# Half-swaps of the last four batches issued from GpSimd's queue instead of the sync queue

## Chip, core and metric

The kernel runs on one NeuronCore of a Trainium2 chip. Its engines work side by side, each through its own instruction queue: TensorE (PE, with PEld for its weight loads), VectorE (DVE), ScalarE (ACT), GpSimd (POOL) and SyncE (SP). SP, ACT and POOL can issue DMAs, and a queue is worked off in order. The metric is the time of one execution in microseconds (us), lower being better; the profile is one such execution, with the time of each instruction.

## Reference

Eight batches of 576 rows and 8 heads of 64 go through a Performer attention; the heads are laid side by side to 512 channels and go through a Hyena block, whose convolution runs over the 576 rows.

```python
def _attn_ref(q, k, v, omega):
    scale = 1.0 / np.sqrt(np.sqrt(D))
    q_s, k_s = (q * scale, k * scale)
    ...
    q_p, k_p = (phi(q_s), phi(k_s))          # 128 random features
    kv = np.einsum('bhsm,bhsd->bhmd', k_p, v)
    z = np.sum(k_p, axis=2)
    num = np.einsum('bhsm,bhmd->bhsd', q_p, kv)
    den = np.einsum('bhsm,bhm->bhs', q_p, z)[..., None] + 1e-06
    return num / den

def _moe_ref(x, w_proj, filter_fft, w_out):
    proj = x @ w_proj                         # 512 -> 3 * 512
    x1, x2, x3 = ...
    X2 = np.fft.rfft(x2, n=S, axis=1)
    H = np.fft.rfft(filter_fft, n=S, axis=0)[None, :, :]
    x2_conv = np.fft.irfft(X2 * H, n=S, axis=1)
    return (x1 * x2_conv * x3) @ w_out
```

## The kernel before

Each batch has 512 rows in four tiles of 128; the 64 rows left over of two batches are worked together, so the batches go in four pairs, `i` from 0 to 3, with `bb` 0 and 1 in a pair. Attention (DVE, ACT and PE) runs ahead of the Hyena stages, and the stages of different batches overlap.

In `hyena()` a pair passes these stages. `fold` makes sums and differences of row chunks, and `project2` multiplies them by the middle third of `wproj`. `forward` takes the Fourier transform by matmuls with tables (`fwb`, `fwa` and others), whose results ScalarE casts to bf16 tiles: `xs` for one part of the spectrum and `sp` for the other. `spectrum` multiplies by the filter on VectorE, and the inverse stage goes back by matmuls that have columns of `xs`, `sp` and `xr` as weights. `gates` makes x1 times x3, and `out` multiplies by `wout`; results are scaled by ScalarE into `osb` (or spare) tiles and stored by SP.

In `sp`, and in `xr` for the left rows of a pair, the two terms of a complex number lie in the two partition halves (0 to 63 and 64 to 127). The complex product therefore needs each half beside the other: `sw` is a copy of `sp` with its halves swapped, and `xw` one of `xr`. Each copy is two DMAs from SBUF to SBUF of 64 partitions: 128 KB for a half of `sw` by the profile's count, 64 KB for a half of `xw`. On VectorE `sp` is multiplied by `hps`, `sw` by `hqs`, and the two are added into `sp`. The first of these overwrites `sp`, so it waits for the swaps too, which read it. `xr`, `xw` work in the same way in `left_spectrum`. There are two buffers of `sw` and of `sp`, one of `xr` and of `xw`.

All instructions are first recorded in a list, then issued in the order of the table `ORDER`, written out in the file, of which every engine gets its own part in that order; the profile puts them all on line 247, the place that issues them, so they are told apart here by tile names. Before the change SP has the loads of a few constants, all swaps and all output stores but one, mixed as `ORDER` has them: a swap that waits for ScalarE's cast holds up the stores behind it, and the reverse. POOL has the loads of q, k, v and the weights, of which the last begins at 137.74 us.

The copies of a pair stand in the functions below.

Of the kernel before, what the change touches and what calls it, by code (L numbers as in the profile page):

```python
# [250 lines left out]
def kernel(  # L251
# [11 lines left out]
    nc = Plan(tc.nc, tc)  # L263
# [31 lines left out]
    def bank():  # L295
        ps = nc.tile(psum, [P, 512], FP32, name="h", bufs=4)
        nc.banks[ps.tensor.name] = ps
        return ps
# [96 lines left out]
    for j in range(2):  # L395
        nc.vector.tensor_scalar_mul(
            out=om2[j * D : (j + 1) * D, :], in0=omt[:D, :MF], scalar1=qk_scale
# [35 lines left out]
    lo64, hi64 = slice(0, 64), slice(64, 128)  # L433
# [619 lines left out]
    def hyena():  # L1053
# [60 lines left out]
        def spectrum(xs, sp, sw):  # L1114
            bt = nc.tile(hy, [P, 2, DM], BF16, name="bt", bufs=2)
            nc.vector.tensor_tensor(
                out=bt[:], in0=xs[:], in1=hb[:].unsqueeze(1).to_broadcast([P, 2, DM]), op=ALU.mult
            )
            nc.vector.tensor_tensor(
                out=xs[:], in0=xs[:], in1=ha[:].unsqueeze(1).to_broadcast([P, 2, DM]), op=ALU.mult  # L1120
            )
            nc.vector.tensor_tensor(
                out=xs[:, 0, :], in0=xs[:, 0, :], in1=bt[:, 1, :], op=ALU.subtract
            )
            nc.vector.tensor_tensor(
                out=xs[:, 1, :], in0=xs[:, 1, :], in1=bt[:, 0, :], op=ALU.add
            )
            nc.vector.tensor_tensor(out=sp[:], in0=sp[:], in1=hps[:, 0:2], op=ALU.mult)
            nc.vector.tensor_tensor(out=sw[:], in0=sw[:], in1=hqs[:, 0:2], op=ALU.mult)
            nc.vector.tensor_tensor(out=sp[:], in0=sp[:], in1=sw[:], op=ALU.add)  # L1130
# [5 lines left out]
        for i in range(B // 2):  # L1136
# [24 lines left out]
            for bb in range(2):  # L1161
# [4 lines left out]
                out=pf[:],  # L1166
# [5 lines left out]
            for j in range(2):  # L1172
                nc.tensor.matmul(
                    out=pf[:],
# [5 lines left out]
            xr = nc.tile(hy, [P, DM], BF16, name="xr", bufs=1)  # L1180
            xw = nc.tile(hy, [P, DM], BF16, name="xw", bufs=1)
            nc.scalar.copy(out=xr[:], in_=pf[:])
            nc.sync.dma_start(out=xw[lo64], in_=xr[hi64])
            nc.sync.dma_start(out=xw[hi64], in_=xr[lo64])

            def left_spectrum():
                nc.vector.tensor_tensor(out=xr[:], in0=xr[:], in1=hps[:, 2], op=ALU.mult)
                nc.vector.tensor_tensor(out=xw[:], in0=xw[:], in1=hqs[:, 2], op=ALU.mult)
                nc.vector.tensor_tensor(out=xr[:], in0=xr[:], in1=xw[:], op=ALU.add)
# [3 lines left out]
            def forward(bb):  # L1193
                nc.at("forward", 2 * i + bb)
                x2 = x2s[bb]
                xs = nc.tile(hy, [P, 2, DM], BF16, name="xs", bufs=2)
                sp = nc.tile(hy, [P, 2, DM], BF16, name="sp", bufs=2)
                xss.append(xs)
                sps.append(sp)
                for m in (2, 3, 0, 1):  # L1200
                    pf = bank()
                    if m < 3:
                        for kt_ in (2, 0, 1):
                            nc.tensor.matmul(
                                out=pf[:],
                                lhsT=fwb[:, 3 * m + kt_, :],
                                rhs=x2[:, kt_, :],
                                start=(kt_ == 2),
                                stop=(kt_ == 1),
                            )  # L1210
                    else:
                        nc.tensor.matmul(
                            out=pf[:], lhsT=fwar[:, bb, :], rhs=x2l[:], start=True, stop=False
                        )
                        nc.tensor.matmul(
                            out=pf[:], lhsT=fwa[:], rhs=x2[:, 3, :], start=False, stop=True
                        )
                    nc.scalar.copy(
                        out=xs[:, m, :] if m < 2 else sp[:, m - 2, :], in_=pf[:]
                    )  # L1220
                    if m == 3:
                        sw = nc.tile(hy, [P, 2, DM], BF16, name="sw", bufs=2)
                        nc.sync.dma_start(out=sw[lo64], in_=sp[hi64])
                        nc.sync.dma_start(out=sw[hi64], in_=sp[lo64])
                spectrum(xs, sp, sw)
                if bb == 0:
                    left_spectrum()
            for bb in range(2):
                forward(bb)
# [8 lines left out]
            for pp, off in ((p1, 0), (p3, 2 * DM)):  # L1238
                for nb in range(CB):
                    for ct in range(CB):  # L1240
                        nc.tensor.matmul(
                            out=pp[:, nb * P : (nb + 1) * P],
# [8 lines left out]
                out=x13l[:].rearrange("p n b s -> p (n b s)"), in0=p3[:], in1=x1[:], op=ALU.mult  # L1251
# [4 lines left out]
            for bb in range(2):  # L1256
                nc.at("inverse", 2 * i + bb)
                xs, sp = xss[bb], sps[bb]
                yt = nc.tile(hy, [P, CB, SM], BF16, name="yt", bufs=2)
                yts.append(yt)  # L1260
                for g in range(CB // 2):
                    gs = slice(2 * g, 2 * g + 2)
                    pa = bank()
                    for u in range(2):
# [3 lines left out]
                            out=dst, lhsT=sp[:, 1, ns], rhs=gta[:, 0:CH], start=True, stop=False  # L1268
                        )
                        nc.tensor.matmul(  # L1270
                            out=dst, lhsT=xr[:, ns], rhs=gns[:, bb, 0:CH], start=False, stop=True
# [8 lines left out]
                    for terms in (  # L1280
# [12 lines left out]
                        for u in range(2):  # L1293
                            ns = slice((2 * g + u) * P, (2 * g + u + 1) * P)
                            for n_, (l_, r_) in enumerate(terms(ns)):
                                nc.tensor.matmul(
                                    out=pv[:, u, 0:EC], lhsT=l_, rhs=r_, start=(n_ == 0), stop=(n_ == 1)
# [5 lines left out]
                        out=yw[:, :, 0], in0=odd[:, :, 0:CH], in1=yc[:, :, 0:CH], op=ALU.add  # L1303
                    )
                    nc.vector.tensor_tensor(
                        out=yw[:, :, 1],
# [5 lines left out]
                        out=yw,  # L1312
# [6 lines left out]
                        out=yt_[:, :, 0:CH], in0=yw[:, :, 0], in1=yw[:, :, 1], op=ALU.add  # L1319
                    )  # L1320
                    nc.vector.tensor_tensor(
                        out=y[:, :, 5::-5],
# [6 lines left out]
                        out=yt[:, gs], in0=x13s[bb][:, gs], in1=yf[:, :, 0:SM], op=ALU.mult  # L1329
                    )  # L1330
                    nc.vector.tensor_tensor(
                        out=ytl[:, gs, bb], in0=x13l[:, gs, bb], in1=yf[:, :, SM:S], op=ALU.mult
# [8 lines left out]
            for bb in range(2):  # L1341
# [5 lines left out]
                for t in order:  # L1347
# [7 lines left out]
                    if final:  # L1355
                        for k_, cs in enumerate((slice(0, 384), slice(384, DM))):
                            n_ = cs.stop - cs.start
                            po = bank()
                            for nb in range(CB):
                                nc.tensor.matmul(  # L1360
                                    out=po[:, 0:n_],
# [8 lines left out]
                            else:  # L1370
                                nc.vector.tensor_scalar(
                                    out=osb,
# [6 lines left out]
                                out=out[b, t * P : (t + 1) * P, cs], in_=osb  # L1379
# [3 lines left out]
                    for nb in range(CB):  # L1383
                        nc.tensor.matmul(
                            out=po[:],
# [12 lines left out]
                    else:  # L1398
                        for j in range(2):
                            nc.sync.dma_start(  # L1400
                                out=out[2 * i + j, SM:S, :], in_=osb[j * SL : (j + 1) * SL, :]
                            )

    attention()
    hyena()
    with tc.nc.allow_low_precision(reason="bf16 factors of both sums"), tc.manual_schedule():
        nc.issue()
# [31 lines left out]
```

## Time and profile before

| | |
|---|---|
| time, median of 3 runs | 261.37 us (260.96 to 261.98) |
| the profiled execution's own time | 261.67 us |
| its span, first to last instruction | 259.9 us |
| mean granted TensorE clock | 0.993 |
| DMAs that POOL issues, software queue q0 | 59616 packets, 17.31 MB |
| DMAs that SP issues, queue q1 | 8280 packets, 12.68 MB |
| swaps issued by SP | 16 of `sw` (median 2.5 us from issue to landing), 8 of `xw` (2.0 us) |
| output stores of 256 KB issued by SP | 24 from `osb`, 2.3 us to landing |

Times in views of the profile count from the first instruction. A line of the timeline gives start, length, engine, source line, operation, tile written and read, and in brackets the idle time before it with what ended it. A line of a stretch gives busy time and number of instructions of each engine in it. The chain of waits is followed back from the last instruction, at each step to what released it.

### The profile page before, as it was taken

What the parts mean: (1) busy time and instruction counts of PE and PEld (TensorE: products, weight loads), DVE (VectorE), ACT (ScalarE), POOL (GpSimd) and SP (SyncE); (2) the same over time, 40 slices, a digit from 0 to 9 for tenths busy, and PEclk for the clock granted to TensorE, in tenths of its full rate; (3) what the DMA queues carried; (4) which work ended last, traced back from release to release, by engine and by line L of the source; (5) the groups of instructions that cost most, each with busy time, mean ns of one, the idle gap of its engine ahead of it and who ended that gap; (6) DMA issues with size and microseconds to landing.
All of it is one profiled execution on the core that took longest, in us unless ns stands there. A gap on an engine that the chain in (4) does not pass through costs nothing.

```text
span 259.9 us, 6421 instructions
## 1 busy us (share of the span) xinstructions
PE 249.1 (96%) x2564; PEld 152.9 (59%) x2564; DVE 219.7 (85%) x501; ACT 214.3 (82%) x334; POOL 62.7 (24%) x87
## 2 busy tenths in 40 slices
PE   8879889999999999999999999999999999999993
PEld 8756656556665654756546755466556755466541
DVE  6799988999755999899999789979988768989870
ACT  5798999999999999878998799898785577665573
POOL 8387746643250441301643000000000000000000
PEclk9997999999999999999999999999999999999999
DMA  6999999999992599932899413010560100342366
GB/s 82 182 190 176 188 197 198 187 180 160 204 140 49 70 132 139 147 37 33 139 64 190 130 62 81 28 55 3 156 177 15 43 0 8 94 124 81 128 226 215
DMA packets 68070, 30.60 MB, mean 118 GB/s; under 512 B 39499, under 2 KB 62536, under 8 KB 68040
## 3 DMA queue, kind: packets, MB, share of 16 engines
q0 software_dynamic: 59616, 17.31, 66.0%
q1 hardware_dynamic: 8280, 12.68, 15.9%
q8 instruction: 20, 0.33, 0.5%
q10 hardware_dynamic: 144, 0.20, 0.2%
q14 instruction: 10, 0.08, 0.1%
HBM read 34.64 MB, written 9.44 MB: 170 GB/s over the span
## 4 chain that ended last, share of the span: by engine, by line
PE 84%; DVE 10%; ACT 3%; issue 1%; DVEq 0%; ACTq 0%
PE h L247 70%; PE a L247 13%; ACT ek L247 1%; DVE vc L247 1%; DVE xb L247 1%; DVE h L247 1%; DVE xf L247 1%; DVE vcl L247 1%; ACT yt L247 1%; DVE mx L247 1%; DVE x L247 1%; DVE xt L247 1%; DVE kt L247 0%; PE h L236 0%; PE a L236 0%
## 5 line engine op out<-in xcount | busy, mean ns | idle before, releaser
L247 PE MATMUL h<-xt,wproj 128*128 128x512 bf16 x256 | 64.1, 379 | 0.0
L247 ACT CAST x<-h 128x512 bf16<-128x512 f32 x68 | 39.2, 598 | 9.4 <-PE h L247 8.9
L247 PEld LDWEIGHTS <-wproj 128*128 128x128 bf16 x384 | 30.3, 98 | 24.4 <-issue 2.8
L247 ACT ACTIVATE osb<-h 128x512 f32<-128x512 f32 (+4 forms) x49 | 27.8, 570 | 8.7 <-PE h L247 7.7
L247 ACT ACTIVATE eqt<-a 128x1024 bf16<-128x1024 f32 x32 | 32.7, 1044 | 1.9 <-PE a L247 1.7
L247 ACT ACTIVATE ek<-a 128x1024 bf16<-128x1024 f32 x32 | 32.3, 1040 | 1.5 <-PE a L247 1.4
L247 PE MATMUL h<-wproj,xf 128*128 128x512 bf16 x128 | 32.1, 379 | 0.3 <-DVE x L247 0.3
L247 PE MATMUL h<-wout,yt 128*128 128x512 bf16 (+2 forms) x132 | 31.4, 373 | 0.0
L247 POOL DMA_DIRECT2D qn<-in_q_dram x26 | 23.3, 905 | 19.8 <-PE a L247 17.1
L247 DVE TENSOR_TENSOR x<-h,x 128x512 bf16<-128x512 f32 x32 | 21.9, 685 | 6.4 <-PE h L247 3.7
L247 DVE TENSOR_TENSOR xb<-a,rden 128x512 bf16<-128x512 f32 x36 | 24.4, 684 | 0.6
L247 PEld LDWEIGHTS <-xf 128*128 128x128 bf16 x134 | 12.4, 98 | 13.6 <-issue 0.9
L247 PEld LDWEIGHTS <-yt 128*128 128x128 bf16 x132 | 12.2, 98 | 12.7 <-issue 0.3
L247 PE MATMUL h<-x,fwb 128*128 128x512 bf16 x72 | 18.7, 379 | 0.0
L247 ACT COPY xt<-h 128x1024 bf16<-128x1024 bf16 x16 | 16.4, 1026 | 1.9 <-PE h L247 1.8
L247 PEld LDWEIGHTS <-eqt 128*128 128x128 bf16 x256 | 11.6, 98 | 5.4 <-DVE xb L247 1.0
L247 DVE COPY kt<-h 128x1024 bf16<-128x1024 bf16 x16 | 10.7, 680 | 4.2 <-PE a L247 2.9
L247 PE MATMUL a<-kv,eqt 128*128 128x65 bf16 x256 | 13.3, 194 | 0.9 <-DVE xb L247 0.9
L247 PE MATMUL a<-om,kt 64*128 64x128 bf16 x256 | 11.8, 218 | 1.6 <-ACT ek L247 0.8
L247 PE MATMUL a<-qt,om 64*128 64x512 bf16 x64 | 11.6, 390 | 1.1 <-ACT ek L247 1.0
L247 ACT COPY qt<-h 128x1024 bf16<-128x1024 bf16 x12 | 12.0, 1020 | 0.6 <-PE h L247 0.4
L247 PE MATMUL h<-gtab,xs 128*128 128x193 bf16 x64 | 12.5, 247 | 0.0
(166 smaller groups left out, 536.6 us busy)
## 6 DMA issues: line engine op xcount, KB each, us to landing
out_dram<-osb SPq DMA_DIRECT2D x24, 256.0 KB, 2.3
vn<-in_v_dram POOLq DMA_DIRECT2D x8, 512.0 KB, 9.3
kn<-in_k_dram POOLq DMA_DIRECT2D x7, 512.0 KB, 9.8
qn<-in_q_dram POOLq DMA_DIRECT2D x24, 128.0 KB, 6.3
sw<-sp SPq DMA_DIRECT2D x16, 128.0 KB, 2.5
wproj<-in_moe_w_proj_dram POOLq DMA_DIRECT2D x3, 512.0 KB, 9.9
qn<-in_q_dram POOLq DMA_DIRECT2D x2, 512.0 KB, 8.2
out_dram<-xf SPq DMA_DIRECT2D x4, 256.0 KB, 2.4
```

What stands on the lines that cost most here:

```text
L247: getattr(real, name)(*args, **kw)
```

## The change

Where the pair's index `i` is 2 or 3 (batches 4 to 7), the swaps of `sp` and of `xr` are issued by GpSimd. Those of batches 0 to 3 stay on SP. These are 8 DMAs of `sw` and 4 of `xw`. They keep their places in `ORDER`; the instructions of PE, VectorE and ScalarE and their order are the same. On POOL the twelve stand behind the last load of inputs, in the order in which SP had them.

```diff
@@ -1180,8 +1180,8 @@
             xr = nc.tile(hy, [P, DM], BF16, name="xr", bufs=1)
             xw = nc.tile(hy, [P, DM], BF16, name="xw", bufs=1)
             nc.scalar.copy(out=xr[:], in_=pf[:])
-            nc.sync.dma_start(out=xw[lo64], in_=xr[hi64])
-            nc.sync.dma_start(out=xw[hi64], in_=xr[lo64])
+            (nc.gpsimd if i >= 2 else nc.sync).dma_start(out=xw[lo64], in_=xr[hi64])
+            (nc.gpsimd if i >= 2 else nc.sync).dma_start(out=xw[hi64], in_=xr[lo64])
@@ -1220,8 +1220,8 @@
                     if m == 3:
                         sw = nc.tile(hy, [P, 2, DM], BF16, name="sw", bufs=2)
-                        nc.sync.dma_start(out=sw[lo64], in_=sp[hi64])
-                        nc.sync.dma_start(out=sw[hi64], in_=sp[lo64])
+                        (nc.gpsimd if i >= 2 else nc.sync).dma_start(out=sw[lo64], in_=sp[hi64])
+                        (nc.gpsimd if i >= 2 else nc.sync).dma_start(out=sw[hi64], in_=sp[lo64])
```

The twelve swaps in the order of both queues, named after their batches: `sw` of batch 4 (two), `xw` of batches 4 and 5 (first half), `sw` of batch 5 (first), `xw` of 4 and 5 (second), `sw` of 5 (second), `xw` of 6 and 7 (first), `sw` of 6 (two), `xw` of 6 and 7 (second), `sw` of 7 (two).

## The prediction

> **What bounds the kernel.** I read the page's busy times first, then the chain of waits from 178 us to the end, the busy times of four stretches in which the moved swaps lie, and then the timelines of the single engines.
>
> ```profile
> PE 249.1 (96%) x2564; PEld 152.9 (59%) x2564; DVE 219.7 (85%) x501; ACT 214.3 (82%) x334; POOL 62.7 (24%) x87
> ```
>
> The chain, as start, length, what:
>
> ```profile
> 183.64 6.38 PE h L247 x35
> ...
> 204.54 51.17 PE h L247 x325
> 255.71 0.04 DVEq L247
> 255.75 0.05 issue
> 255.80 0.29 DVE osb L247
> ```
>
> From 178 us on every piece of it is a matmul until the last one's result is evicted at 255.80; no swap, no VectorE step of the spectrum is in it. A busy PE need not be PE at its peak, so the spacing is checked in PE's timeline:
>
> ```profile
> 227.35 2.75 PE L247 MATMUL h<-wout,yt 128*128 128x512 bf16 x12
> 229.94 1.03 PE L247 MATMUL h<-xt,wproj 128*128 128x512 bf16 x4
> ```
>
> Twelve matmuls of 512 columns take (229.94 - 227.35) / 12 = 0.216 us each from start to start, though one by itself is shown with 0.379 us: they follow each other without a hole. I went through the starts from 180 us to the end in the trace in this way: no matmul begins more than 0.11 us later than its predecessor's columns explain. So there is nothing on PE that an earlier swap could take away. What a later swap can do goes through VectorE:
>
> ```profile
> 180.00:190.00 10.00, 10.00 (x68) 4.83 (x67) 9.78 (x21) 7.92 (x13) 0.00 (x0) 1.00 0.45 139
> 190.00:200.00 10.00, 10.00 (x117) 6.05 (x117) 8.22 (x18) 7.38 (x12) 0.00 (x0) 1.00 0.34 89
> 220.00:230.00 10.00, 10.00 (x48) 4.52 (x47) 9.54 (x22) 6.78 (x13) 0.00 (x0) 1.00 0.30 77
> 230.00:240.00 10.00, 10.00 (x86) 6.51 (x85) 9.01 (x21) 5.49 (x12) 0.00 (x0) 1.00 0.37 123
> ```
>
> The columns are PE, PEld, DVE, ACT, POOL, granted clock, DMA share, GB/s. PE is full in all four, the clock 1.00, POOL empty, and DVE close behind with 9.78, 8.22, 9.54 and 9.01 of 10 us: 0.22, 1.78, 0.46 and 0.99 us of reserve.
>
> **Where the swaps stand now.** SP's timeline:
>
> ```profile
> 186.39 0.47 SPq L247 DMA_DIRECT2D xw<-xr  x1
> 186.90 5.21 SPq L247 DMA_DIRECT2D out_dram<-osb  x5
> 192.21 0.48 SPq L247 DMA_DIRECT2D sw<-sp  x1
> 192.74 0.59 SPq L247 DMA_DIRECT2D xw<-xr  x1
> ```
>
> The second `xw` of batches 4 and 5 stands behind five output stores, 6.35 us after the first one, although the cast of `xr` that both read was over at 186.37. VectorE pays for it once, and once more for the last `sw`, issued from 228.50 on:
>
> ```profile
> 195.14 0.42 DVE L247 TENSOR_TENSOR xw<-xw,hqs 128x512 bf16<-128x512 bf16 x1 [0.82 <-DMA xw<-xr]
> ...
> 232.34 0.69 DVE L247 TENSOR_TENSOR sp<-sp,hps 128x1024 bf16<-128x1024 bf16 x1 [0.42 <-DMA sw<-sp]
> 232.94 0.42 DVE L247 TENSOR_TENSOR xs<-xs,bt 128x512 bf16<-128x512 bf16 x1
> 233.94 0.56 DVE L247 TENSOR_TENSOR bt<-h,xb 128x384 f16<-128x384 f32 x1 [0.57 <-ACT osb L247]
> ```
>
> These 0.82 + 0.42 = 1.24 us are all that VectorE waits for the moved swaps, and PE shows no hole for either.
>
> **What is removed.** Twelve issues of about 0.5 us leave SP. The stores behind them go earlier: the one at 220.03, for instance, stands behind an `xw` for which SP waits 11.0 us for VectorE and 7.4 for ScalarE. Earlier stores free `osb` earlier; the only wait of ScalarE for a store since 178 us is 0.6 us, and it lies at 246.8, behind all swaps. I price this at nothing; its cover is PE's full queue, and without that cover it would be worth those 0.6 us at most.
>
> **What is added.** Twelve issues on POOL, which has nothing since 138.7 us, so each swap queues behind other swaps only. POOL's rows for a load of 64 partitions with one row each (`yt` from the filter) last 0.55 to 0.57 us; I take 0.57. No swap on POOL is in the trace. From issue to landing the nearest rows are its quiet loads of 64 KB:
>
> ```profile
> 125.80 0.68 POOL L247 DMA_DIRECT2D vl<-in_v_dram  x1 [6.97 <-DVE vcl L247]
> ...
> DMA to landing us min/median/max: 3.0/3.0/3.0
> ```
>
> The second line is the answer for that `vl`; the quiet `ql` at 118.14 has 3.4. The swaps themselves take 2.2 to 3.3 on SP. Bounds: 2.2 us, what SP's fastest `sw` has, since a queue can hardly beat the same transfer, and 6.3 us, the median of all `qn` and `ql` loads, mostly with a full queue. I take 3.0, the row nearest in size and in quiet. With it, place by place:
>
> - `sw` of batch 4: issued 181.96 and 182.53 (now 183.60, two stores lie between), landed 185.5. VectorE's first reader begins at 187.36: 1.8 us to spare, more than today.
> - first `xw`, `sw`, second `xw`, `sw` of batches 4 and 5: 186.39, 186.96, 187.53, 188.10. The second `xw` lands at 190.5, the last at 191.1. VectorE could take it at 194.32: the wait of 0.82 us goes. What is late next there is PE: a wait of 0.35 us for a matmul follows at 196.53.
> - `xw` and `sw` of batches 6 and 7: 219.51, then behind the cast of `sp` 221.69 and 222.26, then `xw` at 222.83, landed 225.8. Its reader begins at 226.34: 0.5 us to spare.
> - `sw` of batch 7: 228.50 and 229.07, landed 232.1, against about 232.2 today, where the second issue on SP lasted 1.31 us. The wait of 0.42 us becomes about 0.3.
>
> Sum on VectorE: 1.24 us of waiting become about 0.3, a gain of 0.9 off the path; sum on PE: nothing. With 2.2 us it is the same but for the last 0.3; with 6.3 us the sum is the first rival's. PE does as many matmuls in the same order, so the end moves by 0. The tail (255.71 to 259.9) is an eviction and the last stores, and stays.
>
> The Trainium skill speaks against the change at one point. Advanced Engine Details and Errata, VectorE Performance Modes (Mode Summary), says that VectorE's second SBUF port is shared with GpSimd, and that two-port VectorE instructions and GpSimd's can block each other. By this rule VectorE would lose up to 12 x 0.57 = 6.8 us beside the issues, and the time could grow by some us. The row for it: the four `qn` issues of 126.47 to 129.99 lie beside VectorE's `yt<-x,bt` at 128.20, which takes 0.69 us; the five of the same operation from 181 to 235 us, with POOL empty, have a mean of 0.68. So this trace shows no such loss for DMA issues, and I count none.
>
> **Rivals.** First, slower: POOL's DMAs land late. If each needs the 6.3 us of the busy loads, `sw` of batch 4 lands at 188.8 instead of 187.36 (1.5 late), the second `xw` of the last pair at 229.1 instead of 226.34 (2.8), `sw` of batch 7 at 235.4 instead of 232.34 (3.0), together 7.3 us on VectorE. Its reserve in the four stretches above is 3.45 us and about 1.1 in the next ten; 7.3 - 4.5 = 2.8 us reach PE, 264.2 us for the median. It decides from some 3.7 us to landing on: then the `sw` of batch 7 has used up the 0.57 us that VectorE waits for ScalarE at 233.94, and PE has no result to go on with. For it: VectorE is 95% busy there and POOL's path is longer than SP's. Against: the two quiet loads, with more and smaller packets than a swap has, stay under that point. 15%.
>
> Second, faster: VectorE is the true bound behind a PE that only looks full, and its waits are on the path. Then 0.9 to 1.24 us go, 260.1 to 260.5 us. Against it: the spacing of 0.216 us. 6%.
>
> Third, that the swaps stay behind something on POOL: the issue order has them behind the last load, which begins at 137.74, 44 us before the first of them. With that, nothing is left of it; I keep 3% on the slower side for it and for the port together.
>
> **Numbers.** No change has 76%. The sum is made against the profiled execution, 261.67 us with a span of 259.9; it lies 0.3 us above the median of 261.37. With 0 added I say 261.4. About 0.5%, 1.3 us, is what a measurement of this kernel can tell from no change. The forecast's own range is 260.8 to 262.2, the spread of the three runs and a few tenths for a PE that catches a late bank. To hold the time 8 times in 10 it reaches up into the first rival: 260.6 to 263.0. Faster by over 0.5% needs the whole of the second rival and a little more, so it has 4% of that one's 6, and the other 2 lie within. Slower takes the first and third but for 1% that stays under the bound: 17%. Within: 76 + 2 + 1 = 79%.
>
> **What would show it.** Right: POOL's swaps take 2.5 to 3.4 us to landing; the second `xw` of batches 4 and 5 is issued near 187.5; VectorE's wait at 195.14 is gone; the chain still is matmuls until 255.7. Wrong: landings over 3.7 us, VectorE waiting over 1 us for `sw` or `xw`, holes of PE after 226 us, or `TENSOR_TENSOR` rows longer beside the issues.

## The result and the profile after

The changed kernel takes 263.0 us (median; 262.5 to 263.63) against 261.39 us (260.84 to 262.03) of the kernel before on the same chip: a ratio of 1.0062, with a 95% interval of 1.0048 to 1.0076. It is slower by 0.6%, where no change was forecast with 79%; the time lies at the upper edge of the range, and above the forecast's own range of 260.8 to 262.2. The profiled execution after took 262.95 us with a span of 261.2 us, before 261.67 and 259.9: 1.3 us more in the span, and these are the 1.3 us to be found.

The page's busy times, and its rows for the swaps, after (line, operation, count, then busy time, mean ns and idle time before; in the last two: KB each, us to landing):

```profile
PE 248.5 (95%) x2564; PEld 152.5 (58%) x2564; DVE 220.0 (84%) x501; ACT 214.2 (82%) x334; POOL 69.0 (26%) x99
...
L247 POOL DMA_DIRECT2D sw<-sp x8 | 4.2, 532 | 50.6 <-ACT sp L247 50.5
...
sw<-sp SPq DMA_DIRECT2D x8, 128.0 KB, 2.4
sw<-sp POOLq DMA_DIRECT2D x8, 128.0 KB, 2.6
```

The twelve issues are on POOL, at 0.53 us each, and the median landing is only 0.2 us later than on SP. These averages would let nobody expect 1.3 us. The chain of waits from 178 us to the end shows more:

```profile
234.40 0.05 issue
234.45 18.84 PE h L247 x122
253.28 0.02 issue
...
254.45 2.37 DMA out_dram<-x
256.82 0.00 issue
256.83 0.29 DVE osb L247
```

Before, the last piece of matmuls went back from 255.71 to 204.54; now it is torn at 234.45. (From 253.28 on the view follows a store; that is not what is new, since the last eviction begins 0.10 us after the end of PE's last matmul in both executions.) The waits of that window (total, times, longest) and PE's timeline name the place:

```profile
DVE sp L247 <- DMA sw<-sp: 1.4, 1, 1.4
...
PE h L247 <- DVE xs L247: 0.9, 1, 0.9
```

```profile
233.30 0.25 PE L247 MATMUL h<-gtab,sp 128*128 128x193 bf16 x1
234.45 0.26 PE L247 MATMUL h<-gtab,xs 128*128 128x193 bf16 x1 [0.90 <-DVE xs L247]
```

Matmuls of 193 columns follow each other by 0.08 us here, so the start at 234.45, 1.15 us after its predecessor's, is 1.07 us late (the 0.90 in brackets counts from the predecessor's modelled end). It is the only hole of that size after 178 us. Before, the same matmul started 0.19 us after its predecessor, 0.11 us late:

```profile
233.23 0.25 PE L247 MATMUL h<-gtab,sp 128*128 128x193 bf16 x1
233.42 0.26 PE L247 MATMUL h<-gtab,xs 128*128 128x193 bf16 x1
```

What PE waits for stands in VectorE's timeline:

```profile
231.30 0.69 DVE L247 TENSOR_TENSOR x<-h,x 128x512 bf16<-128x512 f32 x1
233.36 0.69 DVE L247 TENSOR_TENSOR sp<-sp,hps 128x1024 bf16<-128x1024 bf16 x1 [1.38 <-DMA sw<-sp]
233.97 0.42 DVE L247 TENSOR_TENSOR xs<-xs,bt 128x512 bf16<-128x512 bf16 x1
234.97 0.56 DVE L247 TENSOR_TENSOR bt<-h,xb 128x384 f16<-128x384 f32 x1 [0.57 <-issue]
```

The multiplication of `sp` of batch 7 overwrites what the last swap reads, and waits 1.38 us for it (0.42 before). Behind it, in order, stands the last addition of `xs` of batch 6. That addition has nothing to do with the swap, but PE needs its result at once.

Why that swap lands so late is seen in the two queues. First SP before, then POOL and SP after (start, time of the issue or issues):

```profile
228.50 1.83 SPq L247 DMA_DIRECT2D sw<-sp  x2
230.42 4.16 SPq L247 DMA_DIRECT2D out_dram<-osb  x4
```

```profile
228.83 1.04 POOL L247 DMA_DIRECT2D sw<-sp  x2 [5.25 <-ACT sp L247]
```

```profile
229.11 5.54 SPq L247 DMA_DIRECT2D out_dram<-osb  x4
```

On SP the output stores of batch 5 stood behind both halves of the swap, and the first of them left at 230.42. Now SP has nothing to hold it: the store, ready when ScalarE's eviction ends at 229.08, leaves at 229.11, between the two halves on POOL (228.83 and 229.34). The packets of the two queues then overlap, POOL's from 229.92 to 232.80 and SP's, of two stores, from 230.23 to 233.39, and from 231 to 232 the DMA engines are busy all the time (DMA share 1.00, 342 GB/s). By the trace's landings the first store took 2.92 us, and the second half 3.90 us, to 233.24; before, the second half took 3.20, to 232.21. The view of this one DMA, before and after:

```profile
DMA to landing us min/median/max: 3.2/3.2/3.2
```

```profile
DMA to landing us min/median/max: 3.9/3.9/3.9
```

The later landing is the whole hole: 233.24 - 232.21 = 1.03, of which 0.07 lies ahead of the place (ScalarE's cast of `sp` ends at 228.54 instead of 228.47), and PE's start moves from 233.42 to 234.45, by the same 1.03 us.

So the span's 1.3 us are 0.07 us ahead of that cast, 0.96 us at this one place, and 0.25 us behind the last matmul: the last output store is issued by SP 3.78 us before the end of the span in the one and 4.02 us in the other. Its rows before and after:

```profile
256.11 0.33 SPq L247 DMA_DIRECT2D out_dram<-osb  x1
```

```profile
257.15 0.33 SPq L247 DMA_DIRECT2D out_dram<-osb  x1
```

### The profile page after: what moved, and what is told of

It reads as the page before. It is cut to its first block, busy times and chain, and to the rows that moved or that the text cites. A ratio compares the mean times of both kernels' runs of the same rounds, so it can differ in the third digit from the quotient of the medians.

```text
span 261.2 us, 6430 instructions
## 1 busy us (share of the span) xinstructions
PE 248.5 (95%) x2564; PEld 152.5 (58%) x2564; DVE 220.0 (84%) x501; ACT 214.2 (82%) x334; POOL 69.0 (26%) x99
## 5 line engine op out<-in xcount | busy, mean ns | idle before, releaser
L247 POOL DMA_DIRECT2D sw<-sp x8 | 4.2, 532 | 50.6 <-ACT sp L247 50.5
```

The costliest lines, as they stand in the source:

```text
L247: getattr(real, name)(*args, **kw)
```

## Experiments

The theory after the comparison: the loss sits at the last swap alone; it comes from the store that is no longer held behind that swap, and it reaches PE because the `xs` addition stands behind a waiting instruction. The rival: GpSimd's DMAs are late as such, and the last swap is merely where it shows. In what follows "wait" is VectorE's at `sp<-sp,hps` of batch 7, "hole" is PE's late start at `h<-gtab,xs`, "late" is the time from issue to landing of the second half of the last swap, and "tail" is from PE's last matmul to the end of the span, all of the profiled execution. Ratios are to the kernel before, on the same chip.

| | time, us | ratio, 95% interval | wait | hole | late | tail |
|---|---|---|---|---|---|---|
| before | 261.39 | | 0.42 | 0.11 | 3.20 | 4.19 |
| after | 263.0 | 1.0062, 1.0048 to 1.0076 | 1.38 | 1.07 | 3.90 | 4.44 |
| last swap back on SP | 261.32 | 0.9996, 0.9978 to 1.0015 | 0 | 0 | 2.46 | 4.31 |
| only the last swap on POOL | 262.25 | 1.0035, 1.0016 to 1.0055 | 0.84 | 0.53 | 3.34 | 4.32 |
| stores behind the swap on POOL | 261.61 | 1.0002, 0.9986 to 1.0017 | 0 | 0 | 2.30 | 4.56 |
| after, `xs` addition first | 261.55 | 1.0004, 0.9986 to 1.0022 | 1.03 | 0 | 3.88 | 4.45 |
| before, those stores on POOL | 261.85 | 1.0010, 0.9993 to 1.0026 | 0.56 | 0.25 | 3.34 | 4.30 |
| before, store between the halves | 261.73 | 1.0005, 0.9986 to 1.0024 | 0.77 | 0.46 | 2.34 | 4.18 |
| before, `xs` addition first | 261.09 | 0.9984, 0.9964 to 1.0003 | 0 | 0 | 2.95 | 4.19 |
| second store alone behind the swap | 262.67 | 1.0037, 1.0018 to 1.0056 | 0.86 | 0.55 | 3.38 | 4.51 |
| after, again | 263.0 | 1.0061, 1.0040 to 1.0082 | 1.25 | 0.95 | 3.77 | 4.46 |
| only the last swap, again | 262.77 | 1.0045, 1.0027 to 1.0062 | 1.39 | 1.08 | 3.88 | 4.30 |

In two rows (2.46 and 2.34) the view gives no landing for the second half; there it is the last update of that swap's semaphore in the trace. Wherever there is a hole, it is the wait less 0.30 or 0.31 us. And from the end of ScalarE's last cast of `sp` to the end of PE's last matmul all twelve profiles have 27.11 to 27.13 us plus the hole: behind that cast PE loses the hole and nothing else. The cast's own end varies from 227.95 to 228.95 us between executions, whichever kernel it is, so the span of a single profile says little about a difference of this size; in the two above it happens to differ by 0.07 us only.

**Where it sits.** The last swap of the changed kernel goes back to SP; the other ten stay on POOL.

```diff
-  (nc.gpsimd if i >= 2 else nc.sync).dma_start(out=sw[lo64], in_=sp[hi64])
+  (nc.gpsimd if i >= 2 and 2 * i + bb < 7 else nc.sync).dma_start(out=sw[lo64], in_=sp[hi64])
...
```

> The changed kernel with the two sw swaps of batch 7 put back on SP; the other ten swaps stay on POOL. First theory (one place: on SP the swap of batch 7 runs ahead of the store of batch 5 that stands behind it in the queue; on POOL the two transfers run side by side, the second half lands 0.7 us later, and VectorE hands its wait to PE without reserve): the hole of PE near 234.4 shrinks from 1.07 to about 0.1 us and the median falls by 1.0 to 1.3 us, to 261.4 to 262.0. Second theory (POOL's swaps cost time at all their places, through the start and the issue on POOL): ten twelfths of the loss stay, the median is about 262.7.

The hole and the whole loss are gone: 0.9996, apart from the changed kernel's interval. (The second half takes 2.46 us here, against 3.20 in the profile before, in the same order on SP; landings of one order differ between executions.) In SP's timeline the swap is in front of the stores again:

```profile
228.98 1.15 SPq L247 DMA_DIRECT2D sw<-sp  x2
230.22 4.84 SPq L247 DMA_DIRECT2D out_dram<-osb  x4
```

The reverse moves the last swap alone in the kernel before:

```diff
-  nc.sync.dma_start(out=sw[lo64], in_=sp[hi64])
+  (nc.gpsimd if 2 * i + bb == 7 else nc.sync).dma_start(out=sw[lo64], in_=sp[hi64])
...
```

> The kernel before with the two sw swaps of batch 7 alone on POOL, all else on SP. First theory: the whole hole is here, PE waits about 1 us near 234.4, the second half lands 3.9 us after its issue, median 262.4 to 263.0. Second theory: a sixth of the loss, median about 261.6.

Two of the twelve moves make over half of the loss, 0.35%, with a hole of 0.53 us; I had expected about 1 us and 262.4 at least. The two runs together speak against the rival: ten DMAs on POOL cost nothing that is measured, two at this place do. That 262.25 is less than 263.0 left the question whether the other ten add something; both kernels, run again side by side, are told of at the end of this section.

**What makes it late.** In the changed kernel the two stores that used to stand behind the last swap on SP are put behind it on POOL too.

```diff
-  nc.sync.dma_start(out=out[b, t * P : (t + 1) * P, :], in_=osb)
+  (nc.gpsimd if b == 5 and t in (0, 2) else nc.sync).dma_start(out=out[b, t * P : (t + 1) * P, :], in_=osb)
```

> The changed kernel, with the two stores of batch 5 (tiles 2 and 0) that SP issues at 229.11 and 230.02 issued by POOL, behind the last swaps. First theory: without a store beside it the second half of sw of batch 7 lands 2.5 to 2.7 us after its issue (as the undisturbed pairs do: 2.56, 2.57), near 231.9; VectorE's wait falls from 1.38 to 0.1 us, the hole of PE is gone, median 261.4 to 262.0. A third theory (POOL's transfer is slow by itself there, whatever runs beside): landing stays at 3.9 us, median 263.0.

POOL's timeline, and the landings of the two halves:

```profile
228.45 1.04 POOL L247 DMA_DIRECT2D sw<-sp  x2 [5.25 <-ACT sp L247]
229.47 1.14 POOL L247 DMA_DIRECT2D out_dram<-osb  x2
```

```profile
DMA to landing us min/median/max: 2.3/2.3/2.4
```

With all four DMAs on POOL in the old order the swap lands 2.3 us after its issue, and VectorE does not wait:

```profile
230.92 0.68 DVE L247 TENSOR_TENSOR x<-h,x 128x512 bf16<-128x512 f32 x1
231.52 0.68 DVE L247 TENSOR_TENSOR sp<-sp,hps 128x1024 bf16<-128x1024 bf16 x1
232.12 0.41 DVE L247 TENSOR_TENSOR xs<-xs,bt 128x512 bf16<-128x512 bf16 x1
```

From the end of the cast (228.16 here) to the landing of the second half it is 3.10 us, against 232.21 - 228.47 = 3.74 on SP before and 231.98 - 228.95 = 3.03 with the last swap back on SP. So GpSimd's queue alone does not make this swap late; what costs is the store beside it. The ratio is 1.0002. For a pair with no store near it POOL is somewhat slower: from the cast to the second landing of `sw` of batch 6 it is 3.37 us in the changed kernel and 2.93 before.

The changed kernel has a second swap with a store beside it, the half of `sw` that POOL issues at 188.37, 0.16 us after a store of SP. It lands after 3.32 us (3.30 to 3.33 in all six profiles that have it on POOL), where the halves of batches 4 and 6 take 2.2 to 2.6. Three other swaps of POOL's stand close ahead of it as well, so it supports the reading without proving it. VectorE needs it only at 199.91, so there it costs nothing.

Only the second of the two stores is put behind the swap, so that the first still leaves from SP beside it:

```diff
-  nc.sync.dma_start(out=out[b, t * P : (t + 1) * P, :], in_=osb)
+  (nc.gpsimd if b == 5 and t == 0 else nc.sync).dma_start(out=out[b, t * P : (t + 1) * P, :], in_=osb)
```

> The changed kernel with only the second of the two stores (tile 0, issued by SP at 230.02) put behind the swaps on POOL; the first stays on SP at 229.1. If the first store alone makes the delay, the swap lands 3.5 to 3.9 us after its issue and the hole stays at 0.7 to 1.1 us, median 262.6 to 263.0. If both stores share it, landing 3.0 to 3.4, hole 0.3 to 0.6 us, median 262.0 to 262.4.

The first store alone leaves a landing of 3.38 us, a hole of 0.55 and a ratio of 1.0037. Of the 1.6 us between the landings of 2.30 and 3.90 it gives 1.08 in its profile. But the same kernel's hole differs between executions (0.53 and 1.08 for the last swap alone), so that how the two stores share it is not settled: the landing and the hole lie where I had put both stores, the median where I had put the first alone.

**Whether POOL is needed for it.** Two variants of the kernel before leave the swaps on SP. The first puts those two stores on POOL, the edit as above with `t in (0, 2)`:

> The mirror of the change at the one place: the kernel before, all swaps on SP, and the two stores of batch 5 (tiles 2 and 0) issued by POOL, which has nothing else then. If it is enough that a store runs beside the second half of sw of batch 7, whichever queue each has: POOL issues the first store near 229.3, its packets begin near 230.4, the swap's second half lands 0.3 to 1.0 us later than before (near 232.5 to 233.2), PE has a hole of 0.4 to 1.1 us and the median is 261.9 to 262.6. If only a swap on POOL suffers: landing near 232.2, no hole over 0.15 us, median 261.4.

The second leaves all on SP and moves the second half (1275) behind the first store (1208) in the written order:

```diff
-... 1262 1203 1275 1292 1207 1201 1208 1202 1319
+... 1262 1203 1292 1207 1201 1208 1275 1202 1319
```

> The kernel before, all on SP, with the first of those two stores put between the two halves of the swap of batch 7 in SP's order. No POOL, no other queue. If order against the store is the cause: the store waits for ScalarE until 229.0, the second half is issued near 229.5 and its packets stand behind the store's 128, it lands near 232.6 to 233.2, PE has a hole of 0.5 to 1.1 us, median 262.0 to 262.7. If the cause is a property of POOL's path, the hole stays under 0.2 us and the median at 261.5.

```profile
228.20 0.46 SPq L247 DMA_DIRECT2D sw<-sp  x1
228.74 1.14 SPq L247 DMA_DIRECT2D out_dram<-osb  x1
229.93 0.46 SPq L247 DMA_DIRECT2D sw<-sp  x1
```

```profile
232.39 0.69 DVE L247 TENSOR_TENSOR sp<-sp,hps 128x1024 bf16<-128x1024 bf16 x1 [0.77 <-DMA sw<-sp]
```

```profile
233.48 0.26 PE L247 MATMUL h<-gtab,xs 128*128 128x193 bf16 x1 [0.30 <-DVE xs L247]
```

The three rows are of this second variant. The same hole opens without any swap on POOL, 0.46 us by the spacing of the starts, since a store got ahead of the second half. But it opens in another way: the second half is issued only at 229.93, 1.76 us after the end of the cast (0.54 before), and then takes 2.34 us, no more than an undisturbed one. The time is lost in front of the issue and not in the transfer.

With the stores on POOL the second half takes 3.34 us (2.46 to 3.20 in the three profiles that have both on SP, with the stores behind it) and the hole is 0.25 us, less than I had expected and smaller than what the swap suffers in the changed kernel. Neither median can be told from the kernel before, and both lie below what I had expected for a delay.

So a store ahead of the swap in its own queue delays its issue, and a store on the other queue delays its transfer: clearly where POOL has the swap (3.34 to 3.90 us beside stores of SP, 2.30 without), and not shown where SP has it. The store loses too: the first one takes 2.92 us beside the swap in the changed kernel and 2.47 behind it with the last swap back on SP. By which rule the queues share the DMA engines is left open.

**How it reaches PE.** The addition of `xs` (1263) is put ahead of the multiplication that waits (1284), in the changed kernel:

```diff
-1204 1326 1321 1328 1294 1284 1263 1209 ...
+1204 1326 1321 1328 1294 1263 1284 1209 ...
```

> The changed kernel with two neighbours in VectorE's order changed over: the last step of xs of batch 6 (xs added with bt) goes ahead of the step sp times hps of batch 7, which waits for the swap. First theory: the swap still lands 3.9 us after its issue and VectorE still waits some 1 us, but the matmul that needs xs no longer stands behind that wait, so the hole of PE falls from 1.07 to under 0.3 us, median 261.3 to 262.0. If VectorE's lateness reaches PE through the PSUM banks too, 0.4 us or more of the hole comes back a little later, median 262.4 or more.

```profile
231.47 0.41 DVE L247 TENSOR_TENSOR xs<-xs,bt 128x512 bf16<-128x512 bf16 x1
232.91 0.69 DVE L247 TENSOR_TENSOR sp<-sp,hps 128x1024 bf16<-128x1024 bf16 x1 [1.03 <-DMA sw<-sp]
233.52 0.55 DVE L247 TENSOR_TENSOR bt<-h,xb 128x384 f16<-128x384 f32 x1
```

The swap still lands after 3.88 us and VectorE still waits 1.03 us, but PE has no hole and the time cannot be told from before, 1.0004. The `bt` step that follows no longer waits for its input: the wait is taken from one that came after. The late landing by itself costs nothing here; it costs through what stands behind the waiting instruction.

The same exchange in the kernel before:

> The kernel before, with the two neighbours in VectorE's order changed over as in the reordered version of the changed kernel. PE's late start of 0.11 us at 233.4 goes, nothing else: median 261.3 to 261.5, no difference that can be measured. If VectorE's wait of 0.42 us costs PE more than the profile shows, up to 0.4 us less, 261.0.

It takes away the 0.42 us wait and the 0.11 us hole. At 261.09 us, 0.9984 with an interval that reaches 1.0003, it is the fastest version run, and not told apart from the kernel before.

**Whether the other ten swaps add anything.** The changed kernel and the one with the last swap alone, again and on one chip:

> The changed kernel as it is, beside the version with the swap of batch 7 alone on POOL on the same chip. The wait of VectorE less 0.31 us is the hole of PE, as in all runs so far. If the other ten swaps add to the loss, this one again has a hole near 1.07 us, landing near 3.9 us, a span 0.26 us longer behind PE's end than the kernel before, and a median 0.6 to 0.8 us above the other version's. If the two differ by chance alone, their medians lie within 0.3 us and both holes anywhere from 0.5 to 1.1.

> The version with the swap of batch 7 alone on POOL, once more, on the same chip as the changed kernel. If the other ten swaps matter: hole near 0.53 us as in its first run, 4.31 us from PE's end to the end of the span, median 262.2 to 262.4. If they don't: median within 0.3 us of the changed kernel's, of which 0.13 us is the shorter end.

263.0 and 262.77 us, 1.0061 and 1.0045 with intervals that overlap widely; in these executions the hole of the second (1.08) is even the larger. What separates the two kernels in both pairs of profiles is the tail, 4.44 and 4.46 against 4.32 and 4.30 us. So the other ten moves cost about 0.13 us at the tail and nothing else that was found.

## Why the prediction was wrong, point by point

**Right: nothing is to be gained.** The second `xw` of batches 4 and 5 is issued at 187.85 (187.5 foretold), and VectorE's wait at 195.14 is gone. The next thing is late, PE, as said, 1.27 us instead of 0.35:

```profile
194.31 0.41 DVE L247 TENSOR_TENSOR xw<-xw,hqs 128x512 bf16<-128x512 bf16 x1
194.64 0.69 DVE L247 TENSOR_TENSOR xf<-xt 128x1024 bf16<-128x1024 bf16 x1
196.59 0.21 DVE L247 RECIPROCAL rden<-a 128x8 f32<-128x8 f32 x1 [1.27 <-PE a L247]
```

PE is busy for all 10.00 us of 190 to 200, so the 0.82 us bought nothing. The issue of 0.53 us was taken as 0.57. Of a loss at the port that VectorE shares with GpSimd nothing is seen in these instructions either: `sp<-sp,hps` at 229.02, beside POOL's issues, takes 0.69 us, and `sp<-sp,sw` at 230.23 without them 0.69. Whether these are two-port instructions no run shows, so the rule itself stays untested.

**Wrong: "earlier stores free `osb` earlier ... I price this at nothing".** This step failed. For `osb` itself nothing came of it, as said: ScalarE's one wait for a store is 0.6 us after the change too (it ends at 250.04 before, not at the 246.8 that I read). But I looked only at whom an earlier store helps, and not at which transfer it then runs beside; the term put at nothing cost 0.96 us of PE. SP's order had kept the stores off the last swap; taking the swap out of that queue gave the order up. The Trainium skill has the rule that I should have weighed: DMA: Bandwidth & Descriptors, Issuing engines are not separate DMA queues, says that DMAs of ScalarE, SyncE and GpSimd run on the same 16 engines and interleave, whoever starts them. The trace agrees, with 3.90 us to landing beside two stores of the other queue and 2.30 us with the same stores behind it in its own.

**Wrong in size: 3.0 us to landing for every swap.** POOL's other swaps of `sp` land in 2.2 to 2.7 us and once in 3.3, mostly better than taken. The one on which the time depends takes 3.90 and lies beyond the 3.7 us that the first rival gave as its point. That rival had the right place, engine and sign, with 15%; its cause (a slow queue) was wrong, and its price of 2.8 us too, since it let all swaps be late and not one.

**Wrong: the start on POOL.** I had the first half issued at 228.50, as on SP. SP starts 0.02 to 0.03 us after a cast's end, POOL 0.29 us, at each of its five starts behind a cast. That is a term I left out. It is not what made the loss: with the stores behind the swap the same late start is there (228.45 after a cast that ended at 228.16), and VectorE does not wait.

**Wrong: the reserve.** I let 0.57 us of VectorE's wait at 233.94 absorb a late swap. That wait lies behind the `xs` addition, so nothing of it helps PE. The true reserve is 0.31 us, and the 0.42 us wait of the kernel before had used it up: the start 0.11 us late at 233.42 was PE waiting for this very addition. I had that 0.11 us in hand and read it as no hole. From there on each us of the swap was a us of PE.

**Wrong: "the tail ... stays".** It grew by 0.25 us, with the number of DMAs that SP issues, as below.

The sum with the measured terms: landing 1.03 later at a place without reserve (0.07 of it from ahead), and 0.25 at the tail, 1.28 us, for 1.28 between the two profiled executions. The medians differ by 1.61; the other 0.3 us is not accounted for.

## What to carry to other kernels

Before a DMA is moved to another queue, list what stood behind it in the old one and when that will leave now: the queue's order may have been all that kept a bulk store away from a transfer that someone waits for. A late start of 0.1 us on a full engine, right behind a wait of another, tells that there is no reserve at that place: from there on every delay counts in full. Look for independent work standing behind the waiting instruction, and put it in front; here this one exchange took away the loss without touching a DMA.

## What the runs showed of the hardware

GpSimd begins a DMA 0.29 us after the ScalarE cast that it waits for, SyncE 0.02 to 0.03 us. In the trace's packets a half of `sw` is 64 packets of 2048 bytes when SP issues it, and 32 of 4096 when POOL does, and the undisturbed landings are nearly the same: 2.20 and 2.39 us for the two halves of batch 6 on SP, 2.24 and 2.56 on POOL. From the start of an issue on an idle queue to its first packet both take 1.1 us (1.11 at 228.50 on SP, 1.09 at 228.83 on POOL), so that most of what sets POOL back is the later start.

The tail goes with the number of DMAs that were taken off SP: none, 4.18 to 4.19 us; two, 4.30 to 4.32; ten, 4.31; twelve, 4.44 to 4.46; thirteen, 4.51; fourteen, 4.56. Ten are as two, so it seems to repeat after eight, and above the multiple of eight it grows by about 0.06 us for each. That is the spacing at which SP works off its last waits for DMAs, one after another: behind the wait that ends with the last landing one more follows before, and five in the changed kernel. The reading that the last store's semaphore moves to an earlier place in this row fits all twelve profiles, but no run was made for it alone.
